# Cosformer attention feeding a SwiGLU block on one core: ScalarE's share of the last batch's queries begun two slots later, other slots moved, two k-v products in single banks

## The chip, the cores and the metric

One core of a Trainium2 chip runs the whole program in one launch. The time is device microseconds (us) of that core for one execution; smaller is better. The engines are TensorE (PE in the profile, PEld for its weight loads), VectorE (DVE), ScalarE (ACT), GpSimd (POOL) and SyncE (SP). POOL and SP issue the DMA transfers in this program, each through a queue of its own. TensorE writes to PSUM only, here eight banks of 128 partitions x 512 fp32 values.

## The reference, cut to what matters

Eight batches, eight heads, 576 rows, head width 64. Attention without softmax: relu of q and k, each weighted by the cosine and the sine of the row's position, then a gated feed-forward block over 4608 tokens.

```python
def phi(x, c, s):
    r = np.maximum(x, 0.0)
    return np.concatenate([r * c, r * s], axis=-1)
q_p = phi(q, cos_w, sin_w)
k_p = phi(k, cos_w, sin_w)
kv = np.einsum('bhsf,bhsd->bhfd', k_p, v)
z = np.sum(k_p, axis=2)
num = np.einsum('bhsf,bhfd->bhsd', q_p, kv)
den = np.einsum('bhsf,bhf->bhs', q_p, z)[..., None] + 1e-06
x = (num / den)            # to (4608, 512)
g = x @ w_gate             # (512, 1536)
out = (g * (1 / (1 + np.exp(-g)))) * (x @ w_val) @ w_out
```

## The kernel before

**Tiling.** The 4608 tokens are 36 tiles of 128 rows, and four tiles make a group `tg` (0 to 8) of 512 tokens. A batch fills 4.5 tiles, so some tiles straddle two batches. While the feed-forward block of group `tg` runs, the attention for the tiles of group `tg + 1` and the preparation of later batches are put between its matmuls.

**Slots.** A group has 16 slots (`SLOTS`): 12 after the f-tiles of the hidden layer and 4 in its output part, so that slot 80 is slot 0 of group 5. `at(s, f)` files work under a slot, `slot(s)` emits what was filed there (L916 to L921), and each engine takes its instructions in the order of emission. Tables give the slots: `ROW[b]` holds for batch b the slots of its q weighting, of the turn of q, of the k and v work of its four head pairs, and (counted from one group later) of the k-v product; `TILES[tg]` those of the attention tiles; `WSUM` those of four sums over the gate weights (L627). The first three of `ROW[b]` count from `p0 = 16 (b - 2)` (L1063 to L1080).

**A batch.** For each batch from 2 on: `phi_q` (L287) takes one of four head pairs of q through relu on ACT (L276, 128x576) and through a multiplication by the cosine-sine table on DVE (L293, 128x1152) into the single buffer `r_q`; the last batch, b = 7, does all of it on ACT instead, in 18 parts of 128x256 (`phi_q_part`, L299). Two DMA transposes (`qturn_dma`, L322, on SP's queue) turn `r_q` into `phit`. On POOL's queue `load_behind` waits with a small copy (L1038) until `phit` of one batch has landed and then issues the next loads of q, k and v. For each head pair `relu_k` (ACT, L276) and `vmul` (DVE, L303, 128x1152) prepare k and v. `kv_mm` (L342, 72 matmuls at L349) makes the k-v products in two neighbouring banks taken as a pair, and `kv_out2` (L368) copies them to `kv2s`: two copies of 64x260 on ACT, then two on DVE (L373). `kv_free` gives the pair back, one slot later in groups 1 to 4.

**A tile.** `a_tile2` (L460) multiplies `phit` by `kv2s` into a pair of banks (L472), and DVE divides (L486, L495, L499); a DMA transpose on SP's queue (L578) turns the tile into `xT`. In groups 5 to 8 the tiles of the slots 0, 1, 3, 4, 7 and 8 have their DVE part put off: it goes to a list `behind`, which is emptied at two places of the feed-forward code (L692, L701). `kv_out2`'s DVE part goes there too in these groups.

**Feed-forward.** Groups 1 to 4 make gate and value per f-tile (L594, two banks; silu on ACT at L600, product on DVE at L605). Groups 5 to 8 (`GATE`) run `ffn_by_quarters` (L637): per u = 0, 1, 2 seven gate products of quarters (L652) in the banks a, b, c, e, a copy of a to b on ACT (L681), a copy of e to `m7` (L685), two sums on DVE (L691, L700), silus (L658) and value products (L665), with `done()` emitting the next slot. The order of one u is: product a, copy to b, product e, copy to m7, value, slot; product b, sum c, product a, silu a, value, slot; product b, sum m7, silu m7, product c, silu c, value, slot; two products on DVE (L670), product b, silu b, value, a third L670, slot (the last value and slot for u > 0 only). The output part of groups 2 to 8 (`out_by_quarters`, L805) has seven products as well (L826), and ACT and DVE take its banks out (L848, L851, L839; L856, L867, L841). POOL's queue stores (L749).

**Banks.** The helper `take` (L86) picks the bank, or pair, that was used longest ago by its own books; who then waits for whom follows from which bank was picked.

Of the kernel before, what the change touches and what calls it, by code (L numbers as in the profile page):

```python
# [18 lines left out]
def kernel(  # L19
# [10 lines left out]
    nc = tc.nc  # L30
# [3 lines left out]
    J = G // 2  # L34
# [16 lines left out]
    KH = KC // 2  # L51
    GATE = (5, 6, 7, 8)
    AHEAD = 5
    WSUM = (32, 39, 49, 64)
    ROW = {2: ([16, 16, 17, 17], 18, (20, 21, 21, 22), 8), 3: ([12, 13, 14, 15], 18, (20, 20, 21, 21), 6), 4: ([12, 12, 12, 14], 15, (15, 16, 17, 18), 5), 5: ([12, 12, 12, 14], 15, (15, 16, 17, 17), 5), 6: ([6, 8, 11, 12], 14, (13, 14, 14, 17), 3), 7: ([4, 4, 5, 5, 6, 6, 7, 7, 8, 8, 9, 9, 10, 10, 11, 11, 12, 12], 15, (12, 13, 14, 15), 3)}
    TILES = {2: (1, 9, 10, 11), 3: (5, 9, 10, 11), 4: (5, 7, 9, 11), 5: (3, 4, 7, 9), 6: (0, 2, 5, 7), 7: (0, 1, 5, 7), 8: (0, 3, 5, 7)}
    FASTX = {}
    LATE = dict(M=44, V=87, O=131, X=26, x=150, v=(190, 250, 120, 150), e=130, a=90, c=170, b=110, k=120)

    consts = ctx.enter_context(tc.tile_pool(name="consts", bufs=1))  # L60
# [61 lines left out]
    def give_back(hold, late=1):  # L122
        touch(held.pop(hold), late)
# [216 lines left out]
                ps[:, 0:hi - lo].rearrange("p c (e s) -> p c e s", e=2))  # L340

    def kv_mm(b):  # L342
        ps = st[b, "kvps"] = take(2, ("kv", b))
        for j, c in [(j, c) for j in range(J) for c in range(NC)]:
            for i in range(2):
                for e in range(2):
                    es = slice(e * SH, (e + 1) * SH)
                    g = 2 * j + i
                    nc.tensor.matmul(  # L349
                        out=ps[i * D:(i + 1) * D, e, j * 2 * D1:(j + 1) * 2 * D1],  # L350
                        lhsT=raws[b, "k"][es, g, c],
                        rhs=v2s[b == 1][es, g, c, :, 0:D1],
                        start=(c == 0), stop=(c == NC - 1),
                    )
# [12 lines left out]

    def kv_out2(b):  # L368

        ps = st[b, "kvps"][:, :, 0:4 * J * D1 // 2].rearrange("p e (j w x) -> p e j w x", j=J, w=2)  # L370
        def part(w, eng):
            for i in range(2):
                eng(out=kv2s[b % 2][w * D:(w + 1) * D, :, :, i], in_=ps[i * D:(i + 1) * D, :, :, w])  # L373

        part(0, nc.scalar.copy)
        if b - 1 in GATE:
            behind.append(lambda: (part(1, nc.vector.tensor_copy), kv_free(b)))
        else:
            part(1, nc.vector.tensor_copy)
# [187 lines left out]
    def x_turned(t, eng, ks=slice(0, KC)):  # L567
        copy_op(eng, xT_of(t)[:, ks], st.pop(("xt", t, ks.start)))
        give_back(("xt", t, ks.start))

    def x_turn(t, fast=False):
        if t in FASTX:
            at(FASTX[t], lambda: (x_turn_pe(t), x_turned(t, "act")))
        elif fast:
            x_turn_pe(t)
            x_turned(t, "act")
        else:
            nc.sync.dma_start_transpose(out=xT_of(t), in_=st["x", t])  # L578
# [58 lines left out]
    def ffn_by_quarters(tg, slot_of):  # L637

        B11, B12, B21, B22 = x_parts(tg)
        val, gates, count = {}, {}, [0]  # L640

        def bank(nm, **kw):
            return take(1, ("g", tg, nm), **kw).rearrange("p (i x) -> p i x", i=2)

        def free(nm, late):
            give_back(("g", tg, nm), late)

        def product(to, u, a, x, first):
            rows[0] += LATE["M"]
            for i in range(2):  # L650
                for c in range(KH):
                    nc.tensor.matmul(out=to[:, i], lhsT=a[:, c, 2 * u + i], rhs=x[:, :, c],  # L652
                                     start=first and i == 0 and c == 0, stop=c == KH - 1, skip_group_check=True)

        def silu(u, w, j, src):
            if (u, w) not in gates:
                gates[u, w] = sg2p.tile([P, 2, T], BF16, name="sg2")
            nc.scalar.activation(out=gates[u, w][:, :, j * HT:(j + 1) * HT], in_=src, func=AF.Silu, scale=DOWN)  # L658

        def V(u, i, w):  # L660
            fc = 4 * u + 2 * i + w
            val[u, i, w] = take(1, ("v", tg, fc), fills=True)
            rows[0] += LATE["V"]
            for kc in range(KC):
                nc.tensor.matmul(out=val[u, i, w], lhsT=wv_sb[:, kc, fc * P:(fc + 1) * P], rhs=xT[tg][:, :, kc],  # L665
                                 start=(kc == 0), stop=(kc == KC - 1))

        def mul(u, i, w):
            fc = 4 * u + 2 * i + w
            nc.vector.tensor_tensor(out=ht[:, fc], in0=gates[u, w][:, i], in1=val.pop((u, i, w)), op=ALU.mult)  # L670
            give_back(("v", tg, fc), LATE["v"][2 * w + i])

        def done():
            slot_of(count[0])
            count[0] += 1

        for u in range(3):
            a = bank("a", fills=True)
            product(a, u, A11, B11, True)
            b = bank("b", seeded=True)  # L680
            nc.scalar.copy(out=b, in_=a)  # L681
            e = bank("e", fills=True)
            product(e, u, W3, X3, True)
            m7 = m7p.tile([P, 2, HT], FP32, name="m7")
            nc.scalar.copy(out=m7, in_=e)  # L685
            free("e", LATE["e"])
            V(*((u - 1, 1, 1) if u else (u, 0, 0)))
            done()
            product(b, u, W2, X2, False)
            c = bank("c", seeded=True)  # L690
            nc.vector.tensor_tensor(out=c, in0=m7, in1=b, op=ALU.add)  # L691
            while behind:  # L692
                behind.pop(0)()
            product(a, u, A12, B21, False)
            silu(u, 1, 0, a)
            free("a", LATE["a"])
            V(u, 0, 0) if u else V(u, 1, 0)
            done()
            product(b, u, W1, X1, False)
            nc.vector.tensor_tensor(out=m7, in0=m7, in1=b, op=ALU.add)  # L700
            while behind:  # L701
                behind.pop(0)()
            silu(u, 0, 1, m7)
            if u:
                mul(u - 1, 1, 1)
            product(c, u, A22, X4, False)
            silu(u, 0, 0, c)
            free("c", LATE["c"])
            V(u, 1, 0) if u else V(u, 0, 1)
            done()  # L710
            if u == 2:
                token_sum(1, 0, 4)
            mul(u, 0, 0)
            mul(u, 1, 0)
            if u == 2:
                token_sum(3, 4, 6)
            product(b, u, W4, B22, False)
            silu(u, 1, 1, b)
            free("b", LATE["b"])
            if u:  # L720
                V(u, 0, 1)
            mul(u, 0, 1)
            if u == 2:
                token_sum(2, 0, 4)
            if u:
                done()
            if u == 1:
                token_sum(3, 0, 4)
        V(2, 1, 1)
        mul(2, 1, 1)  # L730
        for n in (1, 2):
            token_sum(n, 4, 6)
        done()
# [182 lines left out]
    def at(s, *fns):  # L916
        plan.setdefault(s, []).extend(fns)
# [143 lines left out]
    for b in range(2, B):  # L1061
        s0 = SLOTS * (b - 1)
        p0 = s0 - SLOTS  # L1063
        keng = "dve" if b == 2 else "act"
        phi, turned, weighed, kv_slot = ROW[b]
        if b > 2:
            at(p0 + (3 if b < 5 else 1), lambda b=b: load_behind(b))
        if len(phi) > G:
            for i, s in enumerate(phi):
                at(p0 + s, lambda b=b, i=i: phi_q_part(b, *divmod(i, 2)))  # L1070
        else:
            for g, s in enumerate(phi):
                at(p0 + s, lambda b=b, g=g: phi_q(b, g))
        for g, s in enumerate(weighed):
            at(p0 + s, lambda b=b, g=g: (relu_k(b, g, g + 1, keng), vmul(b, g)))
        for e in range(2):
            at(p0 + turned, lambda b=b, e=e: qturn_dma(b, e))
        at(s0 + kv_slot, lambda b=b: kv_mm(b), lambda b=b: kv_out2(b))
        if b - 1 not in GATE:
            at(s0 + kv_slot + 1, lambda b=b: kv_free(b))  # L1080
    at(SLOTS + 4, a_(8, 0))
    at(SLOTS + 5, a_(8, 1), turn(8))
    for tg in range(2, NTG):
        for i in range(tg == 2, OUT):
            t, s = tg * OUT + i, TILES[tg][i]
            later = tg - 1 in GATE and s in (0, 1, 3, 4, 7, 8)
            at(SLOTS * (tg - 1) + s, lambda t=t, later=later: (a_tile2(t, later), None if later else x_turn(t)))
            if t == 10:
                at(SLOTS * (tg - 1) + s, load_3)
# [50 lines left out]
```

## Time and profile before

The heading figures are the median of four runs and one profiled execution, whose span is from the first to the last instruction.

| | |
|---|---|
| median of 4 runs | 314.5 us (314.02 to 314.64) |
| the profiled execution | 314.02 us, span 312.2 us |
| granted TensorE clock | 1.00 |
| HBM read, written | 37.75 MB, 9.44 MB |
| group 5, from 184.6 to 217.6 us | 33.00 us; PE busy 31.43, DVE 26.60, ACT 22.75 |
| group 6, from 217.6 to 248.9 us | 31.30 us; PE busy 31.30, DVE 24.36, ACT 13.63 |

A row of the timeline gives the start, the length, the engine, the line, the operation, what it writes and reads, how many were merged and, in brackets, the idle time of the engine before and what ended it. The chain of waits follows the end of the program backwards: at each step to what released an instruction, or to the one before it on its engine. Line numbers are those of the kernel before.

### The profile page before, as it was taken

To read this page: it belongs to the slowest core of one execution; us is meant where nothing else is said; L and a number is where in the kernel's file an instruction comes from. 1 tells how busy PE (TensorE), PEld (TensorE's weight loads), DVE (VectorE), ACT (ScalarE), POOL (GpSimd) and SP (SyncE) were. 2 spreads that over 40 slices of the span, in tenths; PEclk is the share of its full clock that TensorE was granted. 3 is DMA by queue.
4 is the path that set the end of the run, shared out by engine and by line. 5 is a ranking of instruction groups with operands and counts; after the bars stand their busy time and mean duration, and the time that the engine had idled before them with its cause. 6 is when DMAs were issued, how large, how long until landed. Compare 5 with 4: busy or idle time off the path is not lost.

```text
span 312.2 us, 6940 instructions
## 1 busy us (share of the span) xinstructions
PE 303.6 (97%) x2768; PEld 197.1 (63%) x2768; DVE 234.8 (75%) x470; ACT 153.5 (49%) x290; POOL 66.0 (21%) x118
## 2 busy tenths in 40 slices
PE   8899999999999999999999999899999999999993
PEld 4597455445445486547654686668667876786683
DVE  7874778697777987587887887898879569855781
ACT  7454545663336355435535455786553255324530
POOL 7854202000521205030503031201300130032000
PEclk9999999999999999999999999999999999999999
DMA  7999998996798997969397979895930051013005
GB/s 257 224 198 197 206 204 142 230 142 96 123 232 120 154 197 111 196 103 195 74 181 95 200 125 181 98 144 84 213 43 17 5 149 36 17 38 100 2 0 135
DMA packets 72977, 41.08 MB, mean 132 GB/s; under 512 B 49905, under 2 KB 69873, under 8 KB 72945
## 3 DMA queue, kind: packets, MB, share of 16 engines
q0 software_dynamic: 24880, 24.91, 45.7%
q1 hardware_dynamic: 47472, 15.21, 31.4%
q10 hardware_dynamic: 592, 0.52, 0.5%
q8 instruction: 21, 0.34, 0.5%
q14 instruction: 12, 0.09, 0.1%
HBM read 37.75 MB, written 9.44 MB: 151 GB/s over the span
## 4 chain that ended last, share of the span: by engine, by line
PE 93%; DVE 3%; ACT 2%; issue 0%; DVEq 0%; ACTq 0%
PE banks L594 33%; PE banks L826 21%; PE banks L665 13%; PE banks L652 11%; PE banks L767 6%; PE banks L349 3%; PE banks L472 2%; PE banks L522 1%; PE banks L453 1%; DVE v L303 1%; DVE ht L670 1%; PE banks L207 1%; PE banks L564 0%; PE banks L396 0%; ACT L239 0%; DVE x L499 0%
## 5 line engine op out<-in xcount | busy, mean ns | idle before, releaser
L600 ACT ACTIVATE sg<-banks 128x512 bf16<-128x512 f32 (+2 forms) x68 | 37.1, 547 | 52.3 <-PE banks L594 49.4
L594 PE MATMUL banks<-xT,wg_sb 128*128 128x512 f16 (+2 forms) x272 | 62.0, 354 | 0.0
L594 PE MATMUL banks<-xT,wv_sb 128*128 128x512 f16 (+2 forms) x272 | 62.0, 354 | 0.0
L605 DVE TENSOR_TENSOR ht<-sg,banks 128x512 f16<-128x512 bf16 (+2 forms) x68 | 41.6, 620 | 19.9 <-PE banks L594 12.7
L749 POOL DMA_DIRECT2D out_dram<-ob x56 | 29.4, 532 | 119.6 <-ACT ob L839 114.7
L665 PE MATMUL banks<-xT,wv_sb 128*128 128x512 f16 x192 | 48.6, 379 | 0.0
L594 PEld LDWEIGHTS <-wv_sb 128*128 128x128 f16 x272 | 26.1, 98 | 26.1
L594 PEld LDWEIGHTS <-wg_sb 128*128 128x128 f16 x272 | 24.8, 98 | 21.5
L826 PEld LDWEIGHTS <-ht 128*128 128x128 f16 x336 | 32.7, 98 | 4.9
L670 DVE TENSOR_TENSOR ht<-sg,banks 128x512 f16<-128x512 bf16 x48 | 31.1, 680 | 3.7 <-ACT sg L658 3.7
L665 PEld LDWEIGHTS <-wv_sb 128*128 128x128 f16 x192 | 18.8, 98 | 13.3
L826 PEld LDWEIGHTS <-sums 128*128 128x128 f16 x252 | 24.6, 98 | 2.9
L658 ACT ACTIVATE sg<-banks 128x512 bf16<-128x512 f32 x36 | 20.4, 588 | 11.8 <-PE banks L652 11.8
L652 PEld LDWEIGHTS <-wgs_sb 128*128 128x128 f16 x192 | 17.9, 98 | 8.3 <-issue 1.5
L652 PE MATMUL banks<-kvt,wgs_sb 128*128 128x256 f16 x144 | 21.6, 273 | 1.2 <-ACT banks L681 0.8
L767 PE MATMUL banks<-wo_sb,ht 128*128 128x512 f16 x96 | 22.7, 379 | 0.0
L499 DVE TENSOR_TENSOR x<-banks,rec 128x512 f16<-128x512 f32 (+1 forms) x32 | 21.6, 674 | 1.3 <-PE banks L453 0.3
L826 PE MATMUL banks<-wo_sb,ht 128*128 128x256 f16 x168 | 20.6, 273 | 0.0
L303 DVE TENSOR_TENSOR v<-raw_v,tab 128x1152 bf16<-128x1152 bf16 x27 | 19.6, 751 | 0.5 <-ACT raw_v L889 0.5
L826 PE MATMUL banks<-wt_sb,sums 128*128 128x256 f16 x168 | 19.5, 273 | 0.0
L826 PE MATMUL banks<-wt_sb,ht 128*128 128x256 f16 x168 | 19.5, 272 | 0.0
L839 ACT ACTIVATE ob<-banks 128x512 f32<-128x512 f32 x14 | 8.4, 597 | 22.0 <-PE banks L826 22.0
(123 smaller groups left out, 407.6 us busy)
## 6 DMA issues: line engine op xcount, KB each, us to landing
out_dram<-ob POOLq DMA_DIRECT2D x56, 128.0 KB, 5.5
raw_k<-in_k_dram POOLq DMA_DIRECT2D x7, 576.0 KB, 6.5
raw_q<-in_q_dram POOLq DMA_DIRECT2D x6, 576.0 KB, 11.6
raw_v<-in_v_dram POOLq DMA_DIRECT2D x6, 576.0 KB, 9.9
wo_sb<-in_moe_w_out_dram POOLq DMA_DIRECT2D x3, 512.0 KB, 12.8
out_dram<-ob SPq DMA_DIRECT2D x11, 128.0 KB, 6.1
wg_sb<-in_moe_w_gate_dram POOLq DMA_DIRECT2D x5, 256.0 KB, 9.3
wv_sb<-in_moe_w_val_dram POOLq DMA_DIRECT2D x5, 256.0 KB, 9.6
```

The costliest lines, as they stand in the source:

```text
L303: nc.vector.tensor_tensor(out=v2s[b == 1][:, g, :, :, 0:D], in0=(first if b == 0 and g == 0 else {"v": raw_of(b, "v")})["v"][:, g].unsquee ...
L499: nc.vector.tensor_tensor(out=st["x", t].rearrange("p (y e d) -> p e y d", e=2, d=D)[:, :, ys], in0=ps[:, :, 0:2 * J * D1].rearrange("p e ...
L594: nc.tensor.matmul(out=st["f", tg, fc, lo][i], lhsT=(wg_sb, wv_sb)[i][:, kc, fs], rhs=xT[tg][:, ts, kc], start=(kc == 0), stop=(kc == KC - 1))
L600: nc.scalar.activation(out=sg[:, 0:n], in_=st["f", tg, fc, lo][0], func=AF.Silu, scale=DOWN)
L605: nc.vector.tensor_tensor(out=ht[:, fc, r:r + n], in0=st.pop(("s", tg, fc, lo))[:, 0:n], in1=ps[1], op=ALU.mult)
L652: nc.tensor.matmul(out=to[:, i], lhsT=a[:, c, 2 * u + i], rhs=x[:, :, c], start=first and i == 0 and c == 0, stop=c == KH - 1, skip_group_ ...
L658: nc.scalar.activation(out=gates[u, w][:, :, j * HT:(j + 1) * HT], in_=src, func=AF.Silu, scale=DOWN)
L665: nc.tensor.matmul(out=val[u, i, w], lhsT=wv_sb[:, kc, fc * P:(fc + 1) * P], rhs=xT[tg][:, :, kc], start=(kc == 0), stop=(kc == KC - 1))
L670: nc.vector.tensor_tensor(out=ht[:, fc], in0=gates[u, w][:, i], in1=val.pop((u, i, w)), op=ALU.mult)
L749: (queues or (nc.sync, nc.sync))[e].dma_start(out=out_v[idx // NC, idx % NC][:, cols], in_=ob_of(t)[e * SH:(e + 1) * SH, cols])
L767: nc.tensor.matmul(out=o_ps[t], lhsT=ht[:, fc, r:r + P], rhs=wo_sb[:, fc], start=(fc == 0), stop=(fc == FC - 1))
L826: nc.tensor.matmul(out=to[i][:, 0] if len(to) == 2 else to[0][:, i], lhsT=a[:, kc, i * P:(i + 1) * P], rhs=b[:, kc], start=first and kc == ...
```

## The change

Six edits, none of which alters what is computed.

- `ROW[7]`: the 18 parts of batch 7's q weighting on ACT go from slots 4 to 12 of group 5 to slots 6 to 14, and its turn from slot 15 to 16.
- The other rows: batch 3's four parts of q go from slots 12, 13, 14, 15 of group 1 to 12, 12, 13, 13, and its first head pair's k and v from slot 4 of group 2 to slot 1; batch 4's parts of q from 12, 12, 12, 14 to 12, 12, 14, 14, its first k and v from slot 15 to 13; batch 5's first k and v from slot 15 to 14; batch 6's third and fourth k and v from slots 14 and 17 to 15 and 18. The turns of batches 4, 5 and 6 are filed one or two slots sooner.
- `WSUM`: the first three sums over the gate weights go from slots 32, 39 and 49 to 29, 38 and 48.
- `TILES`: tile 13 goes from slot 9 of group 2 to slot 8. (Another number changes in an entry that the loop skips.)
- `KVONE`: the k-v products of batches 2 and 5 take two single banks; ACT then copies the one out in four pieces of 64x130, DVE the other, and both banks are given back at once.
- `FASTX`, which was empty, goes; the set of late tiles becomes a table with the same numbers in each entry; and `behind` is emptied at a third place.

```diff
-    WSUM = (32, 39, 49, 64)
-    ROW = {2: ([16, 16, 17, 17], 18, (20, 21, 21, 22), 8), 3: ([12, 13, 14, 15], 18, (20, 20, 21, 21), 6), 4: ([12, 12, 12, 14], 15, (15, 16, 17, 18), 5), 5: ([12, 12, 12, 14], 15, (15, 16, 17, 17), 5), 6: ([6, 8, 11, 12], 14, (13, 14, 14, 17), 3), 7: ([4, 4, 5, 5, 6, 6, 7, 7, 8, 8, 9, 9, 10, 10, 11, 11, 12, 12], 15, (12, 13, 14, 15), 3)}
-    TILES = {2: (1, 9, 10, 11), 3: (5, 9, 10, 11), 4: (5, 7, 9, 11), 5: (3, 4, 7, 9), 6: (0, 2, 5, 7), 7: (0, 1, 5, 7), 8: (0, 3, 5, 7)}
-    FASTX = {}
+    WSUM = (29, 38, 48, 64)
+    ROW = {2: ([16, 16, 17, 17], 18, (20, 21, 21, 22), 8), 3: ([12, 12, 13, 13], 18, (17, 20, 21, 21), 6), 4: ([12, 12, 14, 14], 14, (13, 16, 17, 18), 5), 5: ([12, 12, 12, 14], 14, (14, 16, 17, 17), 5), 6: ([6, 8, 11, 12], 12, (13, 14, 15, 18), 3), 7: ([6, 6, 7, 7, 8, 8, 9, 9, 10, 10, 11, 11, 12, 12, 13, 13, 14, 14], 16, (12, 13, 14, 15), 3)}
+    TILES = {2: (2, 9, 10, 11), 3: (5, 8, 10, 11), 4: (5, 7, 9, 11), 5: (3, 4, 7, 9), 6: (0, 2, 5, 7), 7: (0, 1, 5, 7), 8: (0, 3, 5, 7)}
+    KVONE = (2, 5)
...
     def kv_mm(b):
-        ps = st[b, "kvps"] = take(2, ("kv", b))
+        if b in KVONE:
+            ps = st[b, "kvps"] = [take(1, ("kv", b, e)) for e in range(2)]
+        else:
+            both = st[b, "kvps"] = take(2, ("kv", b))
+            ps = [both[:, e] for e in range(2)]
...
-                        out=ps[i * D:(i + 1) * D, e, j * 2 * D1:(j + 1) * 2 * D1],
+                        out=ps[e][i * D:(i + 1) * D, j * 2 * D1:(j + 1) * 2 * D1],
...
     def kv_out2(b):
+        if b in KVONE:
+            for e, eng in enumerate((nc.scalar.copy, nc.vector.tensor_copy)):
+                ps = st[b, "kvps"][e][:, 0:4 * J * D1 // 2].rearrange("p (j w x) -> p j w x", j=J, w=2)
+                for w in range(2):
+                    for i in range(2):
+                        eng(out=kv2s[b % 2][w * D:(w + 1) * D, e, :, i], in_=ps[i * D:(i + 1) * D, :, w])
+                give_back(("kv", b, e))
+            return
...
             mul(u, 0, 0)
             mul(u, 1, 0)
+            while behind:
+                behind.pop(0)()
...
-        if b - 1 not in GATE:
+        if b - 1 not in GATE and b not in KVONE:
             at(s0 + kv_slot + 1, lambda b=b: kv_free(b))
```

More of the change, by code (lines that the diff above doesn't have):

```diff
@@ L53 @@
     AHEAD = 5
-    WSUM = (32, 39, 49, 64)
-    ROW = {2: ([16, 16, 17, 17], 18, (20, 21, 21, 22), 8), 3: ([12, 13, 14, 15], 18, (20, 20, 21, 21), 6), 4: ([12, 12, 12, 14], 15, (15, 16, 17, 18), 5), 5: ([12, 12, 12, 14], 15, (15, 16, 17, 17), 5), 6: ([6, 8, 11, 12], 14, (13, 14, 14, 17), 3), 7: ([4, 4, 5, 5, 6, 6, 7, 7, 8, 8, 9, 9, 10, 10, 11, 11, 12, 12], 15, (12, 13, 14, 15), 3)}
-    TILES = {2: (1, 9, 10, 11), 3: (5, 9, 10, 11), 4: (5, 7, 9, 11), 5: (3, 4, 7, 9), 6: (0, 2, 5, 7), 7: (0, 1, 5, 7), 8: (0, 3, 5, 7)}
-    FASTX = {}
+    WSUM = (29, 38, 48, 64)
+    ROW = {2: ([16, 16, 17, 17], 18, (20, 21, 21, 22), 8), 3: ([12, 12, 13, 13], 18, (17, 20, 21, 21), 6), 4: ([12, 12, 14, 14], 14, (13, 16, 17, 18), 5), 5: ([12, 12, 12, 14], 14, (14, 16, 17, 17), 5), 6: ([6, 8, 11, 12], 12, (13, 14, 15, 18), 3), 7: ([6, 6, 7, 7, 8, 8, 9, 9, 10, 10, 11, 11, 12, 12, 13, 13, 14, 14], 16, (12, 13, 14, 15), 3)}
+    TILES = {2: (2, 9, 10, 11), 3: (5, 8, 10, 11), 4: (5, 7, 9, 11), 5: (3, 4, 7, 9), 6: (0, 2, 5, 7), 7: (0, 1, 5, 7), 8: (0, 3, 5, 7)}
+    KVONE = (2, 5)
+    LATER = {2: (0, 1, 3, 4, 7, 8), 3: (0, 1, 3, 4, 7, 8), 4: (0, 1, 3, 4, 7, 8), 5: (0, 1, 3, 4, 7, 8), 6: (0, 1, 3, 4, 7, 8), 7: (0, 1, 3, 4, 7, 8), 8: (0, 1, 3, 4, 7, 8)}
     LATE = dict(M=44, V=87, O=131, X=26, x=150, v=(190, 250, 120, 150), e=130, a=90, c=170, b=110, k=120)
@@ L571, in x_turn @@
     def x_turn(t, fast=False):
-        if t in FASTX:
-            at(FASTX[t], lambda: (x_turn_pe(t), x_turned(t, "act")))
-        elif fast:
+        if fast:
             x_turn_pe(t)
@@ L1085 @@
             t, s = tg * OUT + i, TILES[tg][i]
-            later = tg - 1 in GATE and s in (0, 1, 3, 4, 7, 8)
+            later = tg - 1 in GATE and s in LATER[tg - 1]
             at(SLOTS * (tg - 1) + s, lambda t=t, later=later: (a_tile2(t, later), None if later else x_turn(t)))
```

## The prediction

> **What bounds the kernel now.** I read the page's busy shares and its chain, then who waited for whom on PE, then the chain in each place found there, then the timeline around it.
>
> ```profile
> PE 303.6 (97%) x2768; PEld 197.1 (63%) x2768; DVE 234.8 (75%) x470; ACT 153.5 (49%) x290; POOL 66.0 (21%) x118
> PE 93%; DVE 3%; ACT 2%; issue 0%; DVEq 0%; ACTq 0%
> ```
>
> PE is busy 97% of the span and carries 93% of the chain; its clock was granted in full. The change neither adds nor removes a matmul, so it can only win back PE's waits. After 60 us, these are all of PE's waits over 0.15 us:
>
> ```profile
> PE banks L652 <- ACT banks L681: 0.8, 1, 0.8
> PE banks L652 <- DVE x L499: 0.4, 1, 0.4
> PE banks L349 <- DVE ht L670: 0.3, 1, 0.3
> ```
>
> All three lie in group 5. What they cost I take from start to start, since a matmul's end is modelled. The chain at the largest:
>
> ```profile
> 200.00 0.89 PE banks L652 x8
> 200.88 0.04 issue
> 200.92 0.58 ACT sg L658
> 201.50 0.80 ACT r_q L299 x2
> 202.29 0.49 ACT banks L681
> 202.83 1.03 PE banks L652 x8
> ```
>
> Product b of u = 2 cannot begin before the copy from a to b (L681), which stands on ACT behind two parts of batch 7's q and a silu. Timeline, same place:
>
> ```profile
> 198.31 0.91 ACT L299 ACTIVATE r_q<-raw_q,cs_all 128x256 bf16<-128x256 bf16 x2 [1.84 <-DMA xT<-x]
> 199.12 0.61 ACT L658 ACTIVATE sg<-m 128x512 bf16<-128x512 f32 x1
> 200.12 0.89 ACT L299 ACTIVATE r_q<-raw_q,cs_all 128x256 bf16<-128x256 bf16 x2
> 201.57 0.42 PE L472 MATMUL banks<-kv,phit 128*128 128x65 bf16 x8
> 202.83 0.60 PE L652 MATMUL banks<-kvt,wgs_sb 128*128 128x256 f16 x4 [0.84 <-ACT banks L681]
> ```
>
> ACT was idle 1.84 us before the first two parts, until batch 6's turn had landed (at 198.31 POOL's small copy waits for that `phit`, and `r_q` is one buffer). Eight matmuls of a tile take 0.26 to the next (198.28 to 198.53), so product b was due at 201.83: 1.00 us lost. Likewise 0.57 us before the L652 at 191.82 and 0.40 at the k-v product at 193.61 (0.49 beyond the step of a matmul, of which 0.09 is usual there).
>
> **The parts, costed.** All times are of the old execution; from 202 us on everything moves 1 us sooner together. *Batch 7's q, slots 6 to 14.* ACT's row without the six parts of slots 4 to 6: silu of m7 when its sum (L700, 197.18 + 0.69) is done, 197.9; silu c 198.5; silu b when its product ends (199.13), to 199.75; now the first two parts, 0.80 by their pitch (201.50 to 202.29 in the chain), to 200.55; L681 by 200.60 to 201.2, before the 201.83 at which PE asks. DVE's L670s, which waited 0.39 us for a silu, move forward too, to about 201.7. Gain 1.00. From slot 7 on ACT's order is the old one, with four parts more at the end.
>
> Those four: slot 13's pair follows the copy at 213.90 (L839) and is done before the next, bound by PE at 216.52. Slot 14's pair comes behind that: 217.01 to 217.81, then two relus of k with a pitch of 1.17 for both (96.06 to 97.23), L681 from 218.98 to 219.55; PE's product b starts at 219.62. Cost 0, 0.1 if each step slips a little; the cover is the value product and tile that PE has in between.
>
> The turn waits for the last part: 217.97 where it was 212.74, 5.2 us later, and behind it on SP's queue the transposes of tile 28 and 29. Batch 7 is first wanted by the split tile at 233.67:
>
> ```profile
> 120.97 11.15 SPq L322 DMA_TRANSPOSE phit<-r_q  x2
> 133.71 0.18 POOL L1038 COPY hold<-phit 1x2 bf16<-1x2 bf16 x1 [9.76 <-DMA phit<-r_q]
> 153.19 11.26 SPq L322 DMA_TRANSPOSE phit<-r_q  x2
> 167.81 0.77 POOL L1038 COPY hold<-phit 1x2 bf16<-1x2 bf16 x1 [11.64 <-DMA phit<-r_q]
> 181.51 9.24 SPq L322 DMA_TRANSPOSE phit<-r_q  x2
> 198.31 0.17 POOL L1038 COPY hold<-phit 1x2 bf16<-1x2 bf16 x1 [9.69 <-DMA phit<-r_q]
> 233.67 0.45 PE L472 MATMUL banks<-kv,phit 128*64 128x65 bf16 x16
> ```
>
> First issue to POOL's copy: 12.7, 14.6 and 16.8 us for batches 4, 5 and 6; 10.1 and 10.2 for 2 and 3. There is room for 233.6 - 218.0 = 15.6. The stores (8 x 128 KB from 217.41) will start 0.6 us before the turn; for batches 4 and 5 they started 1.2 us before, for 6 they came 2.9 us after. I take 12.7 to 14.6: landed by 230.7 to 232.6, cost 0; at 16.8 it is 1.2. The tiles' transposes now issue near 229 and later; `xT` of group 7 is first used at 248, its sums some 4 us before.
>
> The Trainium skill ("DMA: Bandwidth & Descriptors", Latency and other measured facts) gives DMA transposes an effective 261 GB/s. The DMA view of 119 to 135 us shows 1.18 MB for the pair, which took 12.7 us, 93 GB/s with stores beside it. By the page's figure the pair would need an estimated 4.5 us and the sum would have no risk here; the rows decide, and they leave 1 to 3 us. The same page (Queues, rings and completion order) has each engine take whole packets from its queues in turn, so stores beside the turn slow it, which speaks against moving the turn into the stores; the rows agree in direction (10.1 without, 12.7 to 16.8 with).
>
> *Single banks.* No row has 64x130. By the nearest, 128x128: 278 ns on ACT, 282 on DVE, so four pieces take 1.1 us each side, where two of 64x260 took 0.76 and 0.89. Bounds: half of each old copy (0.75), or no saving at all (4 x 374 = 1.5 ACT, 4 x 428 = 1.7 DVE). But the DVE copies waited 1.19 us for ACT's, since both read the same pair; now both start at 71.2 and end at 72.3 (72.0 to 72.9). The tile at 72.85 ran 0.36 to the next start instead of 0.26: gain 0.10, 0 at the upper bound. In group 4 the tile that needs them asks at 168.0, over 2 us after the copies: 0. The other banks exchange names, and the picker gives group 2 another pairing, whose waits I followed: none ends after PE asks.
>
> *Batch 3.* q's parts: ACT relus of 0.63 four in a row behind the copy at 79.97, DVE's four in pairs, `r_q` done near 86.3 instead of 89.9. DVE to the copy at 87.74: 83.25 + two sums of 0.87, W1 0.87, two q parts 1.34 is 87.2, so L776 is on time. The turn then shares the DMA engines with the load of v (576 KB, issued 80.84, 9.1 us to landing, so 3.6 us of it after k's at 86.2) and the group's stores; it lands 0 to 3.6 us sooner, and the next loads follow. `vmul` of slot 17 now stands on DVE at 91.9, ahead of the L605 of f-tiles 2 and 3. If v and the turn halve the engines from 86.3, v lands at about 93.7, L605 of f-tile 2 ends at 95.1; PE wants its bank at 98.02. Cost 0.
>
> *The rest.* Batch 4's `vmul` before L867 takes 0.75 in place of a q part of 0.75, and v of batch 4 (issued 102.30, 12.7 us) is there at 115.0, before 117.3. W2 ahead of the kv copies makes them end at 103.7; tile 13, one f-tile sooner, asks at 104.7. Batch 5's `vmul` puts L841 0.7 us later; its bank is asked for 4 us after. Batch 6's `vmul` at slot 18 lets L700 go at 189.1 instead of 189.65, but DVE's division of the tile at 190.64 waits for PE (0.31 idle), so the chain to 191.77 and 193.6 stays: both smaller waits remain. Filing the turns sooner changes no order on SP; the third emptying of `behind` finds it empty; POOL's order is the old one. All 0.
>
> **Sum.** 1.00 + 0.10 = 1.1 us. The profiled execution: span 312.2 to 311.1, its 314.02 to 312.9. The median lies 0.5 above it: 313.4.
>
> **Rivals.** *Turn of batch 7 late* (15%): PE waits at the split tile for up to 1.2 us, 313.5 to 314.6, middle 314.1. For it: batch 6's 16.8. Against: stores of that one started later in the turn.
>
> *No effect* (8%): L681 late all the same, through a wait on DVE or a longer ACT row than counted; 314.4. Against: 0.6 us of room.
>
> *More* (5%): the two smaller waits go as well, 0.97 more: 312.4. Against: the row at 190.64.
>
> *Slower: v of batch 3 blocks DVE* (8%). DVE takes its queue in order, so a `vmul` waiting for v holds L605 and with it a bank that PE wants at 98.02. If the whole turn went first, v would land at 86.3 + 10.2 + 3.7 = 100.2; its `vmul` and L605 take 1.4 more: a wait of 3.6 us, 317.0. It decides from landing at 96.6 on, cancels the gain at 97.7, and is slower by over 0.2% from 98.3. Against: queues here have shared the engines (stores and turn at 121 to 131).
>
> **The numbers.** Forecast 64%: 313.4, own range 313.0 to 313.8 for the run scatter of 0.3 and the unknown prices. A difference under 0.2% (0.63 us) can't be told from none. Faster: 0.64 + 0.05 + a quarter of the late turn, 0.73. Same: the rest of it and no effect, 0.19. Slower 0.08. Range 312.6 to 314.5: leaves out the slower case and part of the tails.
>
> **What would show it.** Right: no wait of PE on L681 in group 5, the waits on L499 and L670 unchanged, DVE's copies of batch 2's product beside ACT's, the turn of batch 7 issued about 5 us later against group 6. Wrong: a wait at the split tile on `phit`, at group 6's first product b on L681, or DVE idle on `raw_v` near 92.

## The result and the profile after

The changed kernel takes 313.97 us (median of 53 runs, 313.57 to 315.09). In the same rounds the kernel before took 314.78 (79 runs, 313.07 to 317.36). The ratio is 0.9977, 95% interval 0.9969 to 0.9984: 0.72 us less, between 0.50 and 0.98 by the interval (the medians themselves differ by 0.81). The two profiled executions stand the other way round: 314.39 us with a span of 312.6 after, 314.02 and 312.2 before. Whoever compared the spans alone would get the sign wrong, so each piece of the span has to be put down either to the change or to the one execution.

The page of the changed kernel, busy time and chain by engine (the 3% of DMA is a load at the start):

```profile
PE 303.1 (97%) x2768; PEld 196.8 (63%) x2768; DVE 236.0 (76%) x474; ACT 154.3 (49%) x294; POOL 66.4 (21%) x118
PE 92%; DMA 3%; DVE 2%; SPq 1%; ACT 1%; issue 0%; DVEq 0%; ACTq 0%
```

DVE and ACT each have four more instructions (474 for 470, 294 for 290): the k-v products of two batches, copied out in four pieces for each bank. This count will matter.

Who waited for whom on PE in the changed kernel, all of it that lies behind 60 us:

```profile
PE banks L663 <- DVE x L512: 0.4, 1, 0.4
PE banks L354 <- DVE ht L681: 0.3, 1, 0.3
```

The largest of the three old waits, product b on the copy from a to b, is gone; the other two are as they were (line numbers have grown by 5 to 13). The timeline of the changed kernel at the place shows why:

```profile
198.50 0.17 POOL L1051 COPY hold<-phit 1x2 bf16<-1x2 bf16 x1 [9.34 <-DMA phit<-r_q]
200.19 0.89 ACT L300 ACTIVATE r_q<-raw_q,cs_all 128x256 bf16<-128x256 bf16 x2
201.04 0.57 ACT L692 COPY banks<-banks 128x512 f32<-128x512 f32 x1
202.36 0.60 PE L663 MATMUL banks<-kvt,wgs_sb 128*128 128x256 f16 x4
```

The first parts of batch 7's q now come behind the silus, at 200.19; the copy (L692) starts at 201.04 where it started at 202.29; PE's row has no bracket, so it did not wait.

Next I set the start of PE's n-th matmul after the change against the n-th before (both have 2768). Where the difference jumps, something was gained or lost:

| place, time before | after minus before | what it is |
|---|---|---|
| 53 us, still the start of the program | +0.51 | loads of the start; the profiles of the kernels below lie anywhere from 0 to 0.4 here without fillers at the start |
| 72.97, tile after batch 2's k-v product | -0.10 | single banks |
| 119.99, first matmul of group 3 | +0.10 | PE waits for `xT` of the last tile |
| 202.83, product b of u = 2 in group 5 | -1.00 | the wait that went |
| 274.75 | -0.08 | a gap of DVE, see below |
| last matmul, 307.26 | -0.54 in all | |
| last instruction | +0.4 | so 0.92 lost behind PE's last matmul |

From 53 us on PE gains 1.06 us, which is the sum that was predicted, and nearly all of it is lost again after PE's last matmul. ACT's timeline in the tail, first of the kernel before, then of the changed one ("ACTq" is ACT's sequencer issuing DMAs: besides POOL and SP, ACT issues five stores of the tail itself):

```profile
303.64 0.60 ACT L839 ACTIVATE ob<-banks 128x512 f32<-128x512 f32 x1 [2.02 <-PE banks L826]
304.27 2.00 ACTq L756 DMA_DIRECT2D out_dram<-ob  x2
306.32 0.60 ACT L839 ACTIVATE ob<-banks 128x512 f32<-128x512 f32 x1 [2.08 <-PE banks L826]
```

```profile
303.10 0.60 ACT L852 ACTIVATE ob<-banks 128x512 f32<-128x512 f32 x1 [2.02 <-PE banks L839]
303.73 3.08 ACTq L769 DMA_DIRECT2D out_dram<-ob  x2
306.85 0.60 ACT L852 ACTIVATE ob<-banks 128x512 f32<-128x512 f32 x1 [3.16 <-issue]
```

Two issues of stores took 3.08 us instead of 2.00. The durations of the three issues of this line after 300 us (shortest, middle and longest, in ns), before and after:

```profile
L756 ACTq DMA_DIRECT2D out_dram<-ob x3: 642/642/735, 304.3 to 306.9; - x3
```

```profile
L769 ACTq DMA_DIRECT2D out_dram<-ob x3: 625/637/2362, 303.7 to 307.5; - x3
```

The longest is in both the first of the two, 2.36 us where it was 0.74. ACT was held in it, so its copy out of the last-but-one bank, ready at 305.70 by PE, started at 306.85, with "issue" for a reason: the profile knows nothing that it waited for. The copy's store and the stores behind it end later by as much. Nothing in that stretch of the code was changed.

### The profile page after: what moved, and what is told of

It is laid out like the page before. It is cut to its first block, busy times and chain, and to the rows that moved or that the text cites. A ratio compares the mean times of both kernels' runs of the same rounds, so it can differ in the third digit from the quotient of the medians.

```text
span 312.6 us, 6945 instructions
## 1 busy us (share of the span) xinstructions
PE 303.1 (97%) x2768; PEld 196.8 (63%) x2768; DVE 236.0 (76%) x474; ACT 154.3 (49%) x294; POOL 66.4 (21%) x118
## 4 chain that ended last, share of the span: by engine, by line
PE 92%; DMA 3%; DVE 2%; SPq 1%; ACT 1%; issue 0%; DVEq 0%; ACTq 0%
PE banks L605 33%; PE banks L839 21%; PE banks L676 13%; PE banks L663 11%; PE banks L780 6%; PE banks L354 3%; DMA ht<-in_k_dram 3%; PE banks L485 2%; PE banks L535 1%; SPq L171 1%; PE banks L466 1%; DVE ht L681 1%; PE banks L577 0%; DVE x L512 0%; ACT phit L417 0%
## 6 DMA issues: line engine op xcount, KB each, us to landing
raw_v<-in_v_dram POOLq DMA_DIRECT2D x6, 576.0 KB, 10.2
```

## The experiments

All ratios are to the kernel before, run on the same chip in the same rounds. "Tail" is the time from the start of PE's last matmul to the end of the span.

### The main term, both ways

The kernel before with one row changed, and the changed kernel with that row undone:

```diff
-7: ([4, 4, 5, 5, 6, 6, ... 12, 12], 15, (12, 13, 14, 15), 3)
+7: ([6, 6, 7, 7, 8, 8, ... 14, 14], 16, (12, 13, 14, 15), 3)
```

> The kernel before with one edit: the 18 parts of batch 7's q in slots 6 to 14 of group 5 and its turn at slot 16, as in the changed kernel. Theory (the move of q out of slots 4 and 5 is the whole main term): PE's wait of 1.0 us at the product b of u = 2 near 202 us is gone, the two smaller waits near 191.8 and 193.6 stay, every matmul after it starts 1.0 us sooner, and the time is 0.9 to 1.1 us (0.997) below the kernel before. Rival (the wait is released by other edits, batch 6's vmul or the banks): the wait keeps at least 0.5 us and the gain is under 0.5 us.

> The changed kernel with batch 7's q back in slots 4 to 12 and its turn at slot 15. Theory: the wait near 202 us is back with 0.8 to 1.1 us, ACT is idle before the first part until batch 6's turn has landed, and the kernel is 0.2 to 0.5 us slower than the one before (it keeps the later landings ahead of group 3, and without its main term nothing pays for them; ratio 1.000 to 1.0015). Rival: no wait comes back, and the time stays 0.7 us below the kernel before.

Batch 7's q alone: 313.63 us, ratio 0.9964 (0.9945 to 0.9982), 1.1 us less. In its profile PE's starts jump by 1.00 us at 202.83, both small waits stay, and the tail is 4.86 us. It also has a wait that neither theory had asked for, 1.23 us from start to start near 120, in a part of the program that is instruction for instruction the kernel before:

```profile
PE banks L594 <- DMA xT<-x: 1.1, 1, 1.1
PE banks L652 <- DVE x L499: 0.4, 1, 0.4
```

With the row undone: 315.26 us, ratio 1.0012 (0.9986 to 1.0038), and the wait is back, though with 0.65 us instead of 0.8 to 1.1:

```profile
PE banks L663 <- ACT banks L692: 0.5, 1, 0.5
```

So the row makes the whole term. That the wait came back smaller is no contradiction, but shows what sets it. Four profiles have the old row. I take the time of POOL's small copy, which marks the landing of batch 6's turn, less the shift of that run's PE against the kernel before:

| kernel | landing, less the shift | loss at product b, with the tile ahead of it |
|---|---|---|
| row undone | 198.24 - 0.27 = 197.97 | 0.65 |
| before | 198.31 | 1.00 |
| single banks alone (below) | 198.61 + 0.01 = 198.62 | 1.30 |
| before with fillers (below) | 200.96 - 1.83 = 199.13 | 1.82 |

Landing and loss rise together, one for one, in these four. With the old row, PE's wait was the landing time of a DMA, passed on through ACT; with the new row it is none in every profile. This also fits the spread of the times: standard deviation 0.79 us before, 0.34 after.

### One slot further

```diff
-7: ([6, 6, 7, 7, ... 14, 14], 16, (12, 13, 14, 15), 3)
+7: ([7, 7, 8, 8, ... 15, 15], 17, (12, 13, 14, 15), 3)
```

> The changed kernel with batch 7's q one slot later (slots 7 to 15, the turn filed at slot 17). Theory (the turn of batch 7 has 0.4 us of room in the changed kernel): the turn is issued near 219.7 instead of 217.5, lands 1.8 to 2.5 us later, near 234.5, and PE waits 1.4 to 2.2 us at the split tile near 233. Rival (the stores of group 5 are done by then, the turn runs in 10 us as for batches 2 and 3): it lands by 231 and PE waits for nothing.

One run, 315.04 us; PE's last matmul is 0.78 us later than in the changed kernel. Both theories missed the place. PE, then ACT, in its timeline:

```profile
218.92 0.42 PE L485 MATMUL banks<-kv,phit 128*128 128x65 bf16 x8
219.94 0.60 PE L663 MATMUL banks<-kvt,wgs_sb 128*128 128x256 f16 x4 [0.60 <-ACT banks L692]
```

```profile
217.94 0.90 ACT L300 ACTIVATE r_q<-raw_q,cs_all 128x256 bf16<-128x256 bf16 x2
218.73 0.67 ACT L277 ACTIVATE raw_k<-raw_k 128x576 bf16<-128x576 bf16 x1
219.31 0.58 ACT L692 COPY banks<-banks 128x512 f32<-128x512 f32 x1
```

The last pair of parts now stands ahead of the copy of group 6's u = 0, and PE waits there, 0.76 us from start to start. The turn, filed one slot later, slid behind a tile's transpose on SP's queue and was issued at 223.80 instead of 219.7. It still landed at 233.99, just when PE reached it: with the group's stores landed by 224.5 the pair took 10.2 us, as the rival said, where in the changed kernel it took 15.0. The new row thus sits at its last slot, because of ACT's copy and not because of the turn.

### Batch 3's q

```diff
-3: ([12, 12, 13, 13], 18, (17, 20, 21, 21), 6)
+3: ([12, 13, 14, 15], 18, (17, 20, 21, 21), 6)
```

> The changed kernel with only batch 3's four parts of q back in slots 12, 13, 14, 15 (its vmul slots stay). Theory (starting the turn 3 us sooner puts it beside the load of v and made it land 2 us later): the turn is issued near 90 instead of 86.8, POOL's copy of it is done near 100.3 instead of 102.3, the loads of the next batch and the xT tiles of group 3 land 1 to 2 us sooner, PE's 0.10 us at 120.3 is gone, and the time is 0.1 us below the changed kernel (within what can be measured). Rival (the 2 us are the DMA engines' scatter from run to run): the turn lands at 102 or later although it is issued at 90, and the wait at 120.3 stays.

314.63 us, ratio 0.9989 (0.9969 to 1.0009). The turn was issued at 90.22 and landed at 102.21, and PE lost 0.33 us at 120.5: the rival. My theory of a turn slowed by the load of v falls. Over all profiles with that load order unchanged, the second half of batch 3's turn landed as follows, with PE's loss at the first matmul of group 3:

| turn issued | landed (loss near 120 us) |
|---|---|
| 90.0 to 91.0, old slots | 100.1 (0), 100.6 (0), 102.2 (0.33), 102.5 (1.23), 103.4 (0.88) |
| 86.5 to 87.5, new slots | 99.5 (0), 99.7 (0), 99.6 (0), 101.8 (0.22), 102.1 (0.10), 102.4 (0.87), 102.5 (0.77) |

Issuing it 3.5 us sooner made no difference to the landing that these runs can tell. What does matter is which side of some 101 us it falls: POOL lets the next batch's four loads go on it, and these share the DMA engines with the last tiles' turns. That is a reading so far; `AHEAD` below tests it.

### The single banks alone, and the tail

The kernel before with `KVONE = (2, 5)` and its copies, no slot moved:

```diff
+    KVONE = (2, 5)
...
+        if b in KVONE:
+            for e, eng in enumerate((nc.scalar.copy, nc.vector.tensor_copy)):
...
```

> The kernel before with the single banks for the k-v products of batches 2 and 5 alone (KVONE; no slot is moved). Theory: DVE's copies of batch 2's product start beside ACT's near 71.3 instead of 1.2 us behind them, and the tile in group 1 near 72.9 loses 0.1 us less; nothing else on PE moves, time 0.1 us below the kernel before, which is not told from none (ratio 0.999 to 1.000). Rival (the cheaper release is worth more, or the other pairing of the banks costs): PE's starts differ from the kernel before by more than 0.3 us somewhere after 73 us.

315.78 us, ratio 1.0028 (1.0001 to 1.0054), where 0.999 to 1.000 was expected: slower, by 0.9 us. On PE the theory held, 0.10 us gained at 72.97 and 0.08 at 274.75 (and 0.30 lost from 201.57 on, the old wait with a later landing, in the table above). The loss is behind PE, a tail of 5.77 us for 4.96:

```profile
304.49 2.94 ACTq L769 DMA_DIRECT2D out_dram<-ob  x2
307.48 0.60 ACT L852 ACTIVATE ob<-banks 128x512 f32<-128x512 f32 x1 [3.02 <-issue]
```

I then counted ACT's records in the trace, its sequencer's among them. Before, ACT has 457 and the first store of the tail is number 443, from 0; with the single banks it is number 447 of 461. If the place does it, four instructions of any kind must do the same. I repeated a 128x1 silu of a constant at the start of the program, first in the kernel before:

```diff
+    for _ in range(5):
-    nc.scalar.activation(out=tiny, in_=half_pi, func=AF.Silu)
+        nc.scalar.activation(out=tiny, in_=half_pi, func=AF.Silu)
```

> The kernel before with four more instructions on ACT at the start (a 128x1 silu of a constant, done five times instead of once, before 6.5 us, while ACT waits for loads). Theory (the tail's loss goes with the position in ACT's instruction stream: the four more copies of the single banks push the first store of the last tile to place 447 of ACT's records): with four more instructions that store's issue near 304.3 takes 2.2 to 2.4 us instead of 0.74, the last-but-one copy L839 starts about 0.6 us late, and from PE's last matmul to the end of the span it is 5.8 to 6.0 us instead of 4.9; PE itself is unmoved. Rival (the single banks themselves, their naming of the banks or their order, lengthen the tail): 0.74 us for the issue, and 4.9 us.

One run, 317.5 us. The bank pairs are as before, and the tail has it all the same, 5.80 us, with the first of the two issues at 2.22:

```profile
306.92 2.94 ACTq L757 DMA_DIRECT2D out_dram<-ob  x2
309.91 0.60 ACT L840 ACTIVATE ob<-banks 128x512 f32<-128x512 f32 x1 [3.02 <-issue]
```

(PE itself is 2.65 us later: 0.94 at the start, which the fillers cost although I had taken them to be hidden, 0.88 near 120, 0.82 at the old wait.) The same edit in the changed kernel moves the first store on to number 451:

> The changed kernel with the same four additional instructions on ACT at the start. Theory (position in the stream): place 447 now falls on an instruction near 299 to 300 us, while ACT is idle; all issues of stores take 0.5 to 0.8 us, 4.9 us from the last matmul to the end of the span; 0.9 us less than the changed kernel, 1.6 us below the kernel before (ratio 0.994 to 0.996). Rival (four more instructions only cost): tail 5.9 us as in the changed kernel, ratio 0.9977 or above.

314.00 us, ratio 0.9965 (0.9950 to 0.9980), a little short of the 0.994 to 0.996 expected. The tail is 4.88 us and every issue 0.55 to 0.77. In its profile PE is 0.92 us behind the changed kernel near 9 us, where the fillers cost it, and still 0.65 at 53, so that the cure is partly paid for. Last, the four fillers where ACT is idle, ahead of the tail:

```diff
         b = home("b", nb, seeded=True)
+        for _ in range(4 if last else 0):
+            nc.scalar.activation(out=tiny, in_=half_pi, func=AF.Silu)
```

> The changed kernel, single banks and all, with four more instructions on ACT (a 128x1 silu of a constant) between its last gate silu, which ends near 297, and its copy from a to b near 299, where it is idle. Theory (position in ACT's stream, and nothing else, makes the tail's loss): place 447 falls on a semaphore wait near 300.5; every store's issue takes 0.5 to 0.8 us; 4.9 us from the last matmul to the end of the span instead of 5.9; PE as in the changed kernel, with 0 to 1.25 us lost near 120; ratio to the kernel before 0.993 to 0.996, at or up to 0.2 us below the one with the pairs back. Rival (the four fillers delay the copy and product b behind it): PE loses 0.3 us or more between 299 and 303, ratio 0.996 or above.

313.23 us, ratio 0.9957 (0.9943 to 0.9970). ACT's timeline: the fillers, the copy behind them waiting for PE as ever, and the issues short again.

```profile
297.01 0.91 ACT L861 ACTIVATE tiny<-half_pi 128x1 f32<-128x1 f32 x4
299.51 0.63 ACT L863 COPY banks<-banks 128x256 f32<-128x256 f32 x2 [1.59 <-PE banks L839]
...
304.07 2.00 ACTq L769 DMA_DIRECT2D out_dram<-ob  x2
306.12 0.60 ACT L852 ACTIVATE ob<-banks 128x512 f32<-128x512 f32 x1 [2.08 <-PE banks L839]
```

Four additional instructions that do nothing for the output make the changed kernel 0.6 us faster by the ratios (0.9957 for 0.9977). The two intervals just touch, and this kernel has five executions only; the tail, 4.88 us for 5.88, is the plainer sign. Over all fourteen profiles:

| first store of the tail is ACT's record | profiles | its issue | tail |
|---|---|---|---|
| 443 or 451 | 8 | 0.73 to 0.74 us | 4.86 to 4.96 us |
| 447 | 6 | 2.20 to 2.42 us | 5.76 to 5.96 us |

That the place in ACT's stream makes the loss is shown, for the three places that occurred: it comes with the single banks, with fillers in their stead, and goes with the single banks kept. What the sequencer does there is not shown. The DMA view of the changed kernel from 304.0 to 304.5 us has one packet on a queue of its own kind, "instruction", in the middle of the long issue:

```profile
q14 instruction: 1, 0.01, 5.9%
```

The page has 11 such packets with 0.09 MB, 8 KB each. With the single banks alone one lies between 304.7 and 305.2, with the fillers between 307.1 and 307.6, each within 0.4 us of the start of the long issue; with the late fillers it comes between 300.5 and 301, while ACT has nothing to issue. So a fetch of instructions that holds the issue up is a likely reading. But the kernel before has such a packet in its tail as well, from 308.0 to 308.5 us:

```profile
q14 instruction: 1, 0.01, 3.9%
```

There it starts at 308.11, within the issue of a later store of 64 KB (record 450, from 307.92 us), and that issue took 0.55 us, the shortest of the tail. The other five profiles with the first store at 443 have it at the same place. A packet beside an issue therefore does not make it long by itself, and the views do not say which engine a packet is for: the cause behind place 447 stays open. The Trainium skill ("Runtime: NRT & Kernel Launch", Instruction fetch mechanics) says that an engine refills its instruction memory in blocks of 16 KiB, 256 instructions, and that the cost of crossing a block is mostly hidden. Here the packets on this queue are of 8 KB (those on the other instruction queue of the page, q8, are of 16 KB, 21 with 0.34 MB). If it is the fetch that acts at place 447, it was not hidden there: the issue took 1.6 us more, and 0.92 of them reached the end of the program.

### The pairs back, and two tries to go on

```diff
-    KVONE = (2, 5)
+    KVONE = ()
```

> The changed kernel without the single banks (KVONE empty, so all k-v products in bank pairs again); the slots stay changed. Theory: ACT has four instructions fewer, the tail is 4.9 us again; at group 1's tile the 0.1 us is lost again, and DVE waits 0.4 us near 274 us again for nothing that the profile shows, at its 575th record, which costs PE under 0.1; in all 0.75 us below the changed kernel, ratio to the kernel before 0.995 to 0.996. Rival (the single banks are worth what they were costed at): 0.1 us slower than the changed kernel.

313.24 us (6 runs), ratio 0.9951 (0.9934 to 0.9967): 0.8 us below the changed kernel. Tail 4.89 us; the 0.10 near 73 us is lost again. So is the other near 274, and for a like reason. DVE's row there, of the kernel before and then of the changed one:

```profile
274.00 0.70 DVE L856 SCALAR_TENSOR_TENSOR banks<-ob,banks 128x512 f32<-128x512 f32 x1 [1.45 <-PE banks L826]
```

```profile
273.16 0.70 DVE L869 SCALAR_TENSOR_TENSOR banks<-ob,banks 128x512 f32<-128x512 f32 x1 [1.08 <-PE banks L839]
```

Before, and with the pairs back, this is DVE's record 575 and starts 0.46 us after PE released it; in the changed kernel DVE has two records more, it is record 577, and it starts 0.09 us after its release. So it is in all fourteen profiles: 0.45 to 0.46 us in the four where this instruction is record 575, 0.09 in the ten where it is 573, 574 or 577. 575 is 447 and 128 more. ACT's record 191, which is 256 before 447, is late too: in the kernel before it starts 0.36 us after its release, where 0.02 is the median of ACT's activations that had waited. A step of 128 records fits packets of 8 KB if an instruction has 64 bytes, which is an inference from the step and not a reading.

The next try went for the two smaller waits, on the kernel with the pairs back:

```diff
-6: (0, 2, 5, 7)
+6: (0, 1, 5, 7)
```

> The changed kernel without the single banks, and the second tile of group 5 one slot sooner (slots 0, 1, 5, 7). Theory (both smaller waits of group 5 hang on that tile's division, which stands on DVE behind batch 6's vmul): the division comes ahead of the vmul, 0.9 us sooner, so the bank is free before PE's product asks for it at 191.4; the 0.58 us there and the 0.40 us at the k-v product near 193.4 both go; 1.0 us below the kernel without the single banks, ratio to the kernel before 0.991 to 0.993. Rival (the tile one slot sooner finds its own banks not yet free, or a silu is late next): a new wait of 0.3 us or more on PE between 187 and 195, and at most half of the gain.

313.70 us, ratio 0.9969 (0.9947 to 0.9991): not better than the pairs back alone. On PE 0.51 us is lost by 195 us, not 1.0 won:

```profile
188.53 0.29 PE L485 MATMUL banks<-kv,phit 128*128 128x65 bf16 x4
189.27 0.29 PE L485 MATMUL banks<-kv,phit 128*128 128x65 bf16 x4 [0.46 <-DVE x L512]
...
194.27 0.92 PE L354 MATMUL banks<-v,raw_k 64*64 64x130 bf16 x49 [0.80 <-DVE ht L681]
```

The theory was half right: the wait of 0.58 us before the product near 191.4 is gone. But so was the rival: the tile one slot sooner finds its own second bank still being read by the division of the tile before it (0.61 us from start to start), and the wait at the k-v product has grown from 0.49 to 0.96.

The other went for the loss near 120 us, by taking one of the four loads from behind batch 3's turn:

```diff
-    AHEAD = 5
+    AHEAD = 6
```

> The changed kernel without the single banks, and batch 5's q loaded one group later (AHEAD 6 in place of 5), ahead of batch 5's k and v instead of behind batch 4's. Theory (PE's loss of 0 to 1.25 us at the start of group 3 near 120 us, which came in every profile where batch 3's turn had landed after 101.7 and in none where it had by 100.6, is made by the four loads behind that turn, which share the DMA engines with the last tiles' turns): with three loads the last tiles' xT have landed by 117.5 in any case and PE waits for nothing at 120; in place of it the xT tiles of group 4 land up to 3 us later, near 153, and PE may wait up to 1 us near 153. Rival (the tiles' own chain on DVE sets their landing): the last tile's xT lands at 118.5 or later, as before.

> The changed kernel without the single banks, with the second tile of group 5 one slot sooner and batch 5's q one group later: the two edits are 70 us apart, so the sum of their effects: 1.0 us for the tile, and for the load the mean of 0.4 us that the wait near 120 took in ten profiles, if nothing new comes near 153; ratio to the kernel before 0.990 to 0.992. Rival (the load only moves the wait to group 4): no better than the tile alone.

314.39 us, ratio 0.9992 (0.9973 to 1.0012), and with both edits 314.69, ratio 1.0011 (0.9995 to 1.0026). The last `xT` of group 3 landed at 116.75 and 116.69 us and PE lost nothing at 120, so the loads do set that landing (118.31 is the earliest of the other twelve profiles, 118.63 the one with the pairs back). But the load taken away is now behind batch 4's turn, the last `xT` of group 4 landed at 153.79 instead of 151.10, and PE lost 1.62 and 1.14 us there. The wait of the first of the two:

```profile
PE banks L605 <- DMA xT<-x: 1.5, 1, 1.5
```

The two edits together did not reach either part's hoped gain. The best versions by their medians are the changed kernel with the pairs back (313.24) and the one with the late fillers (313.23), which these runs can't tell apart.

## Why the prediction came out as it did

The forecast was 313.4 us in a range of 312.6 to 314.5, with a chance of 0.73 for faster. The result, 313.97, lies in the range, but 0.57 above the forecast and a little outside its own narrower range. It is faster by 0.23%, where the prediction takes anything under 0.2% for none; the interval, 0.16 to 0.31%, reaches below that. About half of the 0.57 is the starting point: the forecast was taken off the median of four runs, 314.5, and 79 runs gave 314.78. The other half is the gain, 0.81 between the medians where 1.10 was forecast.

**PE bound, three waits.** Right. All that the change did on PE is in the places named, and the two waits that were said to stay stayed.

**Batch 7's q, 1.00.** Right in place, path and size for the profile at hand. It was shown by the row alone. What the step didn't say is that the 1.00 was one throw: 0.65 to 1.82 in four profiles, by the landing of batch 6's turn. The row read as evidence (ACT idle 1.84 us until the turn had landed) says it, if one asks how that landing varies.

**Its costs.** The last pair before group 6's copy cost 0 where 0 to 0.1 was given; with one slot more it was 0.76. The turn of batch 7 took 15.0 us where 12.7 to 14.6 were taken. These two lines are PE's split tile in the changed kernel, and in the one with fillers at the start:

```profile
233.20 0.45 PE L485 MATMUL banks<-kv,phit 128*64 128x65 bf16 x16
```

```profile
234.61 0.64 PE L486 MATMUL banks<-kv,phit 128*64 128x65 bf16 x16
```

In the first the turn had landed at 232.51, 0.7 us ahead. In the second it landed at 234.90, inside the tile, which took 0.64 instead of 0.45. The late turn that was the first rival is real, and cost PE 0.20 us here and 0.29 in the profile with the second tile of group 5 moved; a cost of 0 stood within its cover, but with less room than the 1 to 3 us given. The weight that was given to the rows, against the 4.5 us that were estimated for the pair from the Trainium skill's figure ("DMA: Bandwidth & Descriptors", Latency and other measured facts), was right: 15.0 us beside stores, 10.2 in the kernel with one slot more, where the stores had landed by 224.5.

**Single banks, 0.10.** This is the step that failed, though not in what it costed. The timeline of the changed kernel has the copies of batch 2's product side by side, as forecast:

```profile
71.75 1.10 ACT L380 CAST kv<-banks 64x130 bf16<-64x130 f32 x4 [1.39 <-PE banks L354]
71.78 1.23 DVE L380 CAST kv<-banks 64x130 bf16<-64x130 f32 x4 [0.43 <-PE banks L354]
```

A piece took 263 ns on ACT and 292 on DVE (278 and 282 estimated), and PE gained 0.10 at the tile. The step priced the eight additional instructions by their time where they stand and took its bounds from there (0.10, or 0); any cost elsewhere it put at nothing, without a reason. Their number also shifts every later instruction of ACT's and DVE's streams by four and by two places. On ACT that put the tail's first store at record 447, where its issue took 2.36 us for 0.74 and 0.92 us reached the end; on DVE it moved the instruction at 274 off record 575, so that it started 0.09 us after its release for 0.46, which gave PE 0.08 back. Alone, the single banks are slower by 0.9 us (0.03 to 1.7 by the interval). No row of the old profile prices the 0.92 us, but a sign that the place of an instruction can cost time was in the old trace: the 0.46 us of DVE's record 575 at 274.

**Batch 3 sooner.** "Lands 0 to 3.6 us sooner, and the next loads follow" was too hopeful: it lands in the same scatter of 99.5 to 103.4, and its consequence near 120 us, 0 to 1.23 us lost by chance in the old kernel as in the new, was seen nowhere in the prediction. Of v the cost of 0 was right, with more room than the step had given it: v landed at 90.07, where it had at 89.98 before and where the step allowed for 93.7, and the slower rival had nothing to stand on.

**The rest at 0.** Right as far as the profile of the changed kernel shows: PE's starts do not move there. None of these edits was run alone.

**The sum.** On PE 1.06 us instead of 1.10; behind PE -0.92, which was not in it. That leaves 0.14 in these two profiles, and 0.72 (0.50 to 0.98) was measured over many executions. Scatter fills part of the difference: the old wait cost 1.19 us on the mean of four profiles, 0.2 more than in the one profile that the sum was made from, and the 0.10 lost near 120 us is 0 in other profiles of the new order. That makes 0.43. The rest, 0.07 at least and 0.29 by the middle, stays open: the profiled execution of the kernel before was 0.76 us below its median and that of the changed one 0.42 above its own, so single profiles here are off by as much as the effect. That the time still came out inside the range, with a loss of 0.92 us that nothing in the sum stood for, was in part luck.

## What to carry to other kernels

A wait whose first cause is a DMA landing should be priced as a range, from the landing times of several executions; taking the engine off that landing gains its mean and its spread too. An edit that adds instructions moves all later ones of that engine: after it, look at the tail for an idle time put down to "issue", above all where the engine issues the last stores itself; if it is there, a few more or fewer instructions ahead, at a place where the engine is idle, may cure it, as four did here. And a wait that comes only in some executions (here near 120 us) is found by setting the same place of several profiles side by side, not in one.

## What was not expected of the hardware

The issue of one 128 KB store by ACT took 2.20 to 2.42 us at the 447th record of ACT's stream in six profiles, and 0.73 to 0.74 us at the 443rd or 451st in eight. In three of the six the DMA view was read: it shows an 8 KB packet on the instruction queue beside the long issue, but such a packet also lies beside an issue of 0.55 us in the kernel before. On DVE, one instruction started 0.45 to 0.46 us after its release in the four profiles where it was record 575, and 0.09 us after it in the ten others. Two DMA transposes of a batch's q that were issued 6.3 us later (223.80 for 217.52) landed only 1.5 us later (233.99 for 232.51); the group's eight stores had landed by 224.5 us then, and only by 229.0 in the changed kernel.
